# Packed attention's products grouped by tile shape, and a new order of the last batch, in a fused attention, MLP and expert kernel

## The chip, the cores and the metric

One core of a Trainium2 chip. The metric is device time in microseconds of one execution, all eight batches in one launch; the times given are medians of several executions. About 0.3% is what a measurement of this kernel can tell from no change.

## What is computed

The reference chains three layers over a batch of 8, with 576 tokens and 8 heads of 64 columns.

```python
p_packed = sm_attn(p, k, v)            # 32 packed rows per head
out = sm_attn(q, p_packed, p_packed)   # every token attends to the packed rows
...
h = gelu(x @ w_in); u, v = halves of h
gated = u * (w_sg @ layernorm(v) * g_ln + b_sg)
x = x + gated @ w_out
...
logits = x @ w_gate                    # 4 experts, the best 2 kept
for e in range(4):
    out += gate_e * softmax(causal(x @ wq[e] @ (x @ wk[e]).T / 8)) @ (x @ wv[e]) @ wo[e]
```

`sm_attn` is a softmax attention with its scores divided by the root of 64.

## The kernel before

**Batches overlap.** A batch b goes through `front(b)`: the products v and u of the MLP (lines 658 and 739), from the second attention's probabilities `a2` and from `wp`, which is the packed values times `w_in`. Then `back(b)` has the spatial product vs (L769), the query and key products qk (L825 and L837), values and gate logits vlog (L868, L872) and the gates. Expert attention of batch b runs as steps S0 to S9 (scores and softmax), T0 to T9 (transposes of the probabilities), y0 to y4 (times values) and o0 to o4 (times `w_o`, then stored). S and T are numbered 2j + pr: token tile j, expert pair pr. S8 and S9 are the last 64 tokens of the two pairs, and they read copies that `keep_last_q` makes on GpSimd. A batch's S0 and S2 come in its own `back`, all others run between the products of the next batch.

**The packed attention of batch b + 1** is laid between the products of `back(b)` as steps with letters, each for Q = 0 and 1 (four heads each). K turns keys to columns; s is the first scores with max and exponentials (L391, L478, L480); a transposes these (L494); p is the value product `pp` (L401: full-height tiles of 32 columns; L407: 32 by 32 tiles for the last 64 tokens) and its division; P transposes it (L420) and copies it out; Q joins the queries on GpSimd; r is the second scores (L391 again, tiles of 64 by 32), their softmax on VectorE, GpSimd and ScalarE, and the split of the result in a high and a low part. Every matrix product here is made of such parts, in three passes (`PASSES`).

`wp_mm(b + 1, f)` (L602, tiles of 64 by 32) multiplies the packed values by a half of `w_in`: f = 1 for v, f = 0 for u. `wp_out` copies it to a high part on ScalarE (L618) and a low part on VectorE (L623, in the rows as L85). These take two slots of tag "A" each; the four slots of "A" hold the gated values until the last key product, `qk_gated(b, 3, ...)`, has read them: two for m = 0 and 1, two for m = 2 and 3.

**What sets the order.** For TensorE (PE) and for the DMA queue of SyncE (SP) the order is the order of the program text, by hand. VectorE, ScalarE and GpSimd are ordered by a planner when the kernel is built: by priority, which is the order of the text (`s2_` is 150 places ahead), among the work that it takes to be ready. All PSUM tiles share four double banks (`pd`), given to a new tile when an older one has been read out.

**Loads of the packed attention's v.** Heads 4 to 7 of v (j = 2, 3) were loaded into the two "nat" slots, which hold heads 0 to 3 until `pp(0)` has read them. Four further small DMAs bring the last 64 tokens (`vr`, tag "rem", two slots): `load_nat` asks for one at j = 0 that nobody reads, `load_rest` for one each at Q = 0 and Q = 1, and `load_nat` at j = 2 for another that replaces the second.

```python
def p_(Q):                      # L571
    pp(Q)
    if Q == 0:
        for j in range(2, 4):
            load("v", v, j)
...
qk_gated(b, 3, False)           # L1161, in back
...
wp_out(b + 1, 1)
qk_out(b, 3)
wprime(b + 1, 0)                # wp_mm and wp_out
weights(b + 1, ("qk", "vg"))
```

`wp_mm(b + 1, 1)` stood ahead of this, at the end of `first_back` (batch 0) and of `later_back` (batches 1 to 7).

Of the kernel before, what the change touches and what calls it, by code (L numbers as in the profile page):

```python
# [7 lines left out]
F32 = mybir.dt.float32  # L8
# [9 lines left out]
P = 128  # L18
# [8 lines left out]
def packed_attention_mlp_moe_kernel(  # L27
# [43 lines left out]
    def nat_slot(dt, name):  # L71
        return sb.tile([P, 512], dt, tag="nat", name=name, bufs=NB["nat"])
# [281 lines left out]

    NAT = {}

    def load_nat(name, src, b, j):
        t = nat_slot(F32, name).rearrange("p (h n) -> p h n", h=2)
        off = (b * H + 2 * j) * S * D
        NAT[name, b, j] = t  # L360
        for h in range(2):
            nc.sync.dma_start(t[:, h].rearrange("p (c d) -> p c d", c=4),
                              dap(src, off + h * S * D, [[D, P], [P * D, 4], [1, D]]))
        if j % 2 == 0:
            r = small.tile([P, 2, D], F32, tag="rem", name=name + "r", bufs=2)
            for h in range(2):
                nc.sync.dma_start(r[:, h], dap(src, off + (512 + 32 * h) * D, [[S * D, 4], [D, 32], [1, D]]))
            NAT[name + "r", b, j // 2] = r.rearrange("p h d -> p (h d)")
# [9 lines left out]
    STEP = {}  # L378
    TURN = []

    def tick(n=1):
        for _ in range(min(n, len(TURN))):
            for f in TURN.pop(0):
                f()
# [42 lines left out]
    def p1_steps(b):  # L427
# [12 lines left out]
        def load(name, src, j):  # L440
            load_nat(name, src, b, j)
# [61 lines left out]
        def pp(Q):  # L503
            pp_mm_(b, Q, *s.pop(("a1T", Q)))
            pp_out(b, Q)
# [62 lines left out]
            for j in (2 * Q, 2 * Q + 1):  # L568
                join("q", j)

        def p_(Q):  # L571
            pp(Q)
            if Q == 0:
                for j in range(2, 4):
                    load("v", v, j)

        def s2_(Q):
            with tc.high_priority(offset=150):
                s2(Q)
                split_a2(b, Q)  # L580

        for n, fn in (("K", K), ("s", s1), ("Q", Q_), ("a", a1T), ("p", p_), ("P", ppT), ("r", s2_)):
            for Q in range(2):
                STEP[b, f"{n}{Q}"] = lambda fn=fn, Q=Q: fn(Q)
        return steps
# [25 lines left out]
    def wp_mm(b, f):  # L611
        pt = ST[b]["wpp", f] = pd("wp")
        per_head(b, pt, 512, w_of(b, f"in{f}"))
# [193 lines left out]
    def qk(b, i):  # L807
        qk_mm(b, i)
        qk_out(b, i)
# [3 lines left out]
        qk_gated(b, i, True)  # L813
        qk_packed(b, i, False)

    def qk_gated(b, i, first):
        s = ST[b]
        if first:
            s["qkp", i] = pd("qk")[:, :, :HALF]
        o = s["qkp", i]  # L820
        cols = slice(i * P, (i + 1) * P)
        for m in range(4):
            for x, y in PASSES:
                for h in range(2):
                    nc.tensor.matmul(o[:, h, :], W["w_qk"][y][:, m, cols], s["g", m][x][:, hs(h)],  # L825
                                     start=first and (m, x, y) == (0, 0, 0), stop=not first and (m, x, y) == (3, 1, 0))

    def qk_packed(b, i, first):
        s = ST[b]
        if first:  # L830
            s["qkp", i] = pd("qk")[:, :, :HALF]
        o = s["qkp", i]
        cols = slice(i * P, (i + 1) * P)
        for Q in range(2):
            for x, y in PASSES:
                for h in range(2):
                    nc.tensor.matmul(o[:, h, :], s["bd", Q][y][:, cols], s["a2", Q][x][:, hs(h)],  # L837
                                     start=first and (Q, x, y) == (0, 0, 0), stop=not first and (Q, x, y) == (1, 1, 0))

    def qk_out(b, i):  # L840
        s = ST[b]
        o = s.pop(("qkp", i))
        hi, lo = s["qk", i] = [slot("D", F32R, name="qk") for _ in range(2)]
        if i < 2:
            nc.scalar.activation(two(hi), o, AF.Copy, scale=0.125)  # L845
            nc.vector.scalar_tensor_tensor(two(lo), o, 0.125, two(hi).bitcast(F32), op0=OP.mult, op1=OP.subtract)
        else:
            nc.scalar.activation(two(hi), o, AF.Copy)
            lo_part(nc.vector, two(lo), o, two(hi))
# [236 lines left out]
    def first_back(b, do_all):  # L1086
        tick(len(TURN))
        do_all("K0")
        qk_gated(b, 0, True)
        do_all("s0 K1")  # L1090
        qk_gated(b, 2, True)
        do_all("s1")
        bdw(b)
        weights(b + 1, ("in1", "in0"))
        do_all("a0")
        qk_packed(b, 0, False)
        qk_out(b, 0)
        do_all("a1 p0 Q0")
        qk_packed(b, 2, False)
        qk_out(b, 2)  # L1100
        keep_last_q(b, 0)
        do_all("P0")
        vlog(b, VT[2])
        do_all("p1 r0 Q1 P1")
        vlog(b, VT[1])
        do_all("r1")
        wp_mm(b + 1, 1)
        ahead(b + 2)

    def later_back(b, go, do_all):  # L1110
        go("S1 S3")
        vs_tile(b, 0)
        vs_tile(b, 1)
        go("T1 T2 y0 S5 S4")
        vs_tile(b, 2)
        go("T3 o0 y1 T5 T4 S6 S7")
        vs_tile(b, 3)
        tick(len(TURN))
        if b + 1 < B:
            STEP.pop((b + 1, "f"))()  # L1120
        go("o1 y2")
        bdw(b)
        weights(b + 1, ("in1", "in0"))
        qk(b, 0)
        do_all("T6 o2 T7 K0 S8 S9 K1")
        keep_last_q(b, 0)
        qk(b, 2)
        do_all("y3 s0 s1 T8 T9 o3 a0 a1 y4 p0 Q0 Q1 o4 P0")
        vlog(b, VT[1])
        do_all("p1 r0 P1")  # L1130
        vlog(b, VT[2])
        do_all("r1")
        if b + 1 < B:
            wp_mm(b + 1, 1)
        if b + 2 < B:
            ahead(b + 2)

    def back(b, go):
        def do_all(names):

            for n in names.split():
                if (b + 1, n) in STEP:
                    STEP.pop((b + 1, n))()
                elif n[0] in "STyo":
                    go(n)

        if b:
            later_back(b, go, do_all)
        else:
            first_back(b, do_all)  # L1150
        nxt = attention(b)
        vlog(b, VT[0])
        tick()
        gates(b)
        qk(b, 1)
        keep_last_q(b, 1)
        tick()
        qk_packed(b, 3, True)
        tick()
        nxt("S0 S2" if b + 1 < B else "S8 S6")  # L1160
        qk_gated(b, 3, False)  # L1161
        tick()
        if b + 1 == B:
            qk_out(b, 3)
            return nxt
        wp_out(b + 1, 1)
        qk_out(b, 3)
        wprime(b + 1, 0)
        weights(b + 1, ("qk", "vg"))
        if b == 0:  # L1170
            for j in range(2):
                prep_w_o(j)
        return nxt
# [261 lines left out]
    with tc.manual_schedule(engines={ET.PE, ET.SP}):  # L1435
        go = back(0, attention(-1))
        for b in range(1, B):
            front(b, go)
            go = back(b, go)
        go("T8 S9 S7 T6 S4 T9 y4 S5 T7 o4 y3 S2 T4 S3 o3 T5 y2 S0 T2 S1 T3 o2 y1 T0 T1 o1 y0 o0")  # L1440


# [29 lines left out]
```

## Time and profile before

| | us |
|---|---|
| median of 3 runs (852.71 to 855.26) | 852.88 |
| the profiled execution, its device time | 852.21 |
| its span, first to last instruction | 850.4 |
| TensorE busy | 809.0 |
| VectorE busy | 583.6 |
| ScalarE busy | 432.8 |
| GpSimd busy | 227.0 |

The profiled execution is 0.67 below the median, and its device time is 1.8 above its span. Matmuls overlap in a row of the timeline: the cost of a group on TensorE is read from its start to the start of the next group, and not from its length. A row with an idle time in brackets names what ended it.

### The profile page before, as it was taken

To read this page: it belongs to the slowest core of one execution; us is meant where nothing else is said; L and a number is where in the kernel's file an instruction comes from. 1 tells how busy PE (TensorE), PEld (TensorE's weight loads), DVE (VectorE), ACT (ScalarE), POOL (GpSimd) and SP (SyncE) were. 2 spreads that over 40 slices of the span, in tenths; PEclk is the share of its full clock that TensorE was granted. 3 is DMA by queue.
4 is the path that set the end of the run, shared out by engine and by line. 5 is a ranking of instruction groups with operands and counts; after the bars stand their busy time and mean duration, and the time that the engine had idled before them with its cause. 6 is when DMAs were issued, how large, how long until landed. Compare 5 with 4: busy or idle time off the path is not lost.

```text
span 850.4 us, 19209 instructions
## 1 busy us (share of the span) xinstructions
PE 809.0 (95%) x7517; PEld 693.3 (82%) x7517; DVE 583.6 (69%) x1358; ACT 432.8 (51%) x983; POOL 227.0 (27%) x301
## 2 busy tenths in 40 slices
PE   5788989899999999999999999999999999999987
PEld 3456778789789888899789888898789888898965
DVE  5999445887488845876488745875489746875275
ACT  3665332665347542765347542765346542764255
POOL 2457422403322331403322331403322331300000
PEclk9999999999999999999999999999999999999999
DMA  9976886417655366528565476618563372000001
GB/s 255 275 193 166 220 250 166 131 59 207 137 154 125 95 201 139 168 47 228 121 160 113 100 195 136 163 55 237 121 159 106 95 202 84 26 13 27 19 1 57
DMA packets 172565, 114.99 MB, mean 135 GB/s; under 512 B 119290, under 2 KB 153338, under 8 KB 169660
## 3 DMA queue, kind: packets, MB, share of 16 engines
q1 hardware_dynamic: 165500, 112.19, 50.2%
q10 hardware_dynamic: 6976, 1.58, 0.9%
q8 instruction: 59, 0.97, 0.5%
q14 instruction: 30, 0.25, 0.1%
HBM read 69.18 MB, written 29.63 MB: 116 GB/s over the span
## 4 chain that ended last, share of the span: by engine, by line
PE 72%; DMA 11%; DVE 8%; SPq 3%; issue 2%; ACT 2%; POOL 1%; ACTq 0%; DVEq 0%; POOLq 0%
PE vs L769 12%; PE qk L825 9%; PE vlog L868 6%; PE o L1035 5%; PE u L739 5%; PE y L1004 5%; PE v L658 5%; PE qk L837 5%; DMA qp<-turned_q 4%; PE sc L921 4%; PE aTp L975 4%; PE vlog L872 3%; PE wp L602 2%; DMA w_in<-kept_in 1%; SPq L465 1%
## 5 line engine op out<-in xcount | busy, mean ns | idle before, releaser
L769 PE MATMUL vs<-w_sg,vnh 128*128 128x288 f32 x512 | 91.6, 301 | 1.5 <-ACT vs L82 1.5
L472 POOL COPY kT<-kp 128x576 uint16<-128x576 uint16 x56 | 51.1, 987 | 156.0 <-DMA kp<-turned_k 156.0
L825 PE MATMUL qk<-gh,w_qk 128*128 128x288 f32 x512 | 90.6, 299 | 0.0
L934 ACT ACTIVATE at<-sc,nm 128x256 f32<-128x256 f32 (+3 forms) x128 | 66.2, 525 | 39.5 <-DVE nm L925 34.6
L769 PEld LDWEIGHTS vs<-w_sg,vnh 128*128 128x128 f32 x512 | 74.5, 188 | 8.3 <-issue 3.3
L825 PEld LDWEIGHTS qk<-gh,w_qk 128*128 128x128 f32 x512 | 74.7, 188 | 4.7 <-issue 3.8
L82 ACT ACTIVATE aT<-aTp 128x512 f32<-128x512 f32 (+4 forms) x160 | 59.2, 434 | 21.7 <-PE aTp L975 21.2
L868 PE MATMUL vlog<-w_vg,gh 128*128 128x260 f32 (+1 forms) x320 | 61.1, 288 | 0.0
L1004 PE MATMUL y<-aT,v 128*64 128x128 f32 (+2 forms) x960 | 57.2, 262 | 0.8 <-ACT aT L82 0.8
L1004 PEld LDWEIGHTS y<-aT,v 128*64 128x64 f32 (+1 forms) x960 | 46.3, 136 | 13.3 <-issue 8.1
L938 DVE TENSOR_SCALAR at<-at,sm,gw 128x256 f32<-128x256 f32 (+3 forms) x128 | 55.3, 474 | 2.0
L676 POOL TENSOR_TENSOR rstd<-rstd,mhalf 128x1 f32<-128x1 f32 x40 | 35.5, 895 | 77.9 <-DVE rstd L672 74.5
L769 PE MATMUL vs<-w_sg,vnl 128*128 128x288 f32 x256 | 54.8, 296 | 1.0 <-POOL vnl L85 1.0
L472 POOL COPY qT<-qp 128x576 uint16<-128x576 uint16 x56 | 42.6, 833 | 47.2 <-DMA qp<-turned_q 47.1
L825 PE MATMUL qk<-gl,w_qk 128*128 128x288 f32 x256 | 54.9, 296 | 0.2 <-DVE gl L85 0.2
L855 POOL CAST last_q<-qk 64x64 fp32r<-64x64 f32 x64 | 14.9, 232 | 149.6 <-ACT qk L845 77.0
L925 DVE TENSOR_REDUCE nm<-sc 128x2 f32<-128x256 f32 (+3 forms) x64 | 52.7, 823 | 1.9
L1035 PE MATMUL o<-w_o,y 128*128 128x512 f32 x192 | 51.7, 404 | 1.4 <-ACT a L480 0.9
L868 PEld LDWEIGHTS vlog<-w_vg,gh 128*128 128x128 f32 (+1 forms) x320 | 47.7, 178 | 6.5 <-PE s L391 5.9
L874 ACT ACTIVATE v<-vlog 128x512 f32<-128x512 f32 (+1 forms) x24 | 12.6, 523 | 74.9 <-PE vlog L872 74.9
L837 PE MATMUL qk<-a2h,bdq 128*128 128x288 f32 x256 | 45.6, 301 | 0.0
L868 PE MATMUL vlog<-w_vg,gl 128*128 128x260 f32 (+1 forms) x160 | 45.1, 282 | 0.0
(234 smaller groups left out, 1972.0 us busy)
## 6 DMA issues: line engine op xcount, KB each, us to landing
w_in<-kept_in SPq DMA_DIRECT2D x14, 1024.0 KB
w_qk<-kept_qk SPq DMA_DIRECT2D x8, 1024.0 KB
out_dram<-ot SPq DMA_DIRECT2D x32, 256.0 KB
turned_k<-kx SPq DMA_DIRECT2D x28, 288.0 KB
turned_q<-qx SPq DMA_DIRECT2D x28, 288.0 KB
kp<-turned_k SPq DMA_DIRECT2D x56, 144.0 KB
qp<-turned_q SPq DMA_DIRECT2D x56, 144.0 KB
v<-in_v_dram SPq DMA_DIRECT2D x56, 128.0 KB
```

Of the source, the lines that this page charges most:

```text
L82: nc.scalar.activation(o, i, AF.Copy, scale=scale)
L472: nc.gpsimd.tensor_copy(w[:, i], t[:, i].rearrange("p h n -> p (h n)"))
L658: nc.tensor.matmul(pt, s["a2", Q][x][:, c * P:(c + 1) * P], wp_part(b, 1, y, Q), start=n == 0, stop=n == 5)
L769: nc.tensor.matmul(pt[:, h, :], s["vn", c][x][:, cols], w_sg[y][:, c, hs(h)], start=(c, x, y) == (0, 0, 0), stop=False)
L825: nc.tensor.matmul(o[:, h, :], W["w_qk"][y][:, m, cols], s["g", m][x][:, hs(h)], start=first and (m, x, y) == (0, 0, 0), stop=not first an ...
L837: nc.tensor.matmul(o[:, h, :], s["bd", Q][y][:, cols], s["a2", Q][x][:, hs(h)], start=first and (Q, x, y) == (0, 0, 0), stop=not first and ...
L868: nc.tensor.matmul(pt[:n, ci, :260], s["g", m][x][:, c * P:c * P + n], W["w_vg"][y][:, m, :], start=(m, x, y) == (0, 0, 0), stop=False)
L925: nc.vector.tensor_reduce(nm, pt[:, :, :L], axis=AX.X, op=OP.max, negate=True)
L934: nc.scalar.activation(ats[e][:, :L], pt[:, e, :L], AF.Exp, bias=nm[:, e:e + 1], accum_out=sm[:, e:e + 1])
L938: nc.vector.tensor_scalar(ats[e][:, :L], ats[e][:, :L], sm[:, e:e + 1], s["w"][:, j, 2 * pr + e:2 * pr + e + 1], op0=OP.mult, op1=OP.mult)
L1004: nc.tensor.matmul(pt[64 * e:64 * e + 64, pr * w:pr * w + w], s["v2"][:m, c, col:col + D], s["aT", pr, e, j][c][:m, :], start=c == 0, stop ...
L1035: nc.tensor.matmul(pt, ys[:, pr, x, :], W["w_o"][y][:, pr, :], start=i == 0, stop=i == 5)
```

## The change

- v of heads 4 to 7 goes to a slot of tag "a" (three slots, which hold expert probabilities, and in the start raw weights). It is a step of its own, V: after K1 in batch 0, and after T8 and T9 in the others.
- p1 directly follows p0 on TensorE in the batches after the first (Q0 and Q1 are GpSimd's), and P1 follows P0. In batch 0 p1 stays behind vlog of the last tile, and P1 follows it at once. r0 and r1 follow each other, behind vlog of tiles 2 and 3.
- s0 and s1 come before y3.
- `wp_mm` for f = 1 and f = 0 follow each other in the middle of the last key product, between its parts m = 0, 1 and m = 2, 3, with `wp_out` of f = 1 ahead of the second part and that of f = 0 behind the product.
- S0 and S2 come before the packed part of the last key product, not behind it.
- Last batch: S8 comes before qk 1, S6 before and S4 behind the packed part of the last key product, and the items behind it go in another order.

```diff
--- before.py
+++ after.py
@@ -354,8 +354,8 @@
 
     NAT = {}
 
-    def load_nat(name, src, b, j):
-        t = nat_slot(F32, name).rearrange("p (h n) -> p h n", h=2)
+    def load_nat(name, src, b, j, t=None):
+        t = (nat_slot(F32, name) if t is None else t).rearrange("p (h n) -> p h n", h=2)
         off = (b * H + 2 * j) * S * D
         NAT[name, b, j] = t
         for h in range(2):
@@ -568,18 +568,19 @@
             for j in (2 * Q, 2 * Q + 1):
                 join("q", j)
 
-        def p_(Q):
-            pp(Q)
-            if Q == 0:
-                for j in range(2, 4):
-                    load("v", v, j)
+        def V_():
+            t = slot("a", name="v")
+            for j in range(2, 4):
+                load_nat("v", v, b, j, t[:, (j - 2) * 512:(j - 1) * 512])
+
+        STEP[b, "V"] = V_
 
         def s2_(Q):
             with tc.high_priority(offset=150):
                 s2(Q)
                 split_a2(b, Q)
 
-        for n, fn in (("K", K), ("s", s1), ("Q", Q_), ("a", a1T), ("p", p_), ("P", ppT), ("r", s2_)):
+        for n, fn in (("K", K), ("s", s1), ("Q", Q_), ("a", a1T), ("p", pp), ("P", ppT), ("r", s2_)):
             for Q in range(2):
                 STEP[b, f"{n}{Q}"] = lambda fn=fn, Q=Q: fn(Q)
         return steps
@@ -813,13 +814,13 @@
         qk_gated(b, i, True)
         qk_packed(b, i, False)
 
-    def qk_gated(b, i, first):
+    def qk_gated(b, i, first, ms=range(4)):
         s = ST[b]
         if first:
             s["qkp", i] = pd("qk")[:, :, :HALF]
         o = s["qkp", i]
         cols = slice(i * P, (i + 1) * P)
-        for m in range(4):
+        for m in ms:
             for x, y in PASSES:
                 for h in range(2):
                     nc.tensor.matmul(o[:, h, :], W["w_qk"][y][:, m, cols], s["g", m][x][:, hs(h)],
@@ -1087,7 +1088,7 @@
         tick(len(TURN))
         do_all("K0")
         qk_gated(b, 0, True)
-        do_all("s0 K1")
+        do_all("s0 K1 V")
         qk_gated(b, 2, True)
         do_all("s1")
         bdw(b)
@@ -1101,10 +1102,9 @@
         keep_last_q(b, 0)
         do_all("P0")
         vlog(b, VT[2])
-        do_all("p1 r0 Q1 P1")
+        do_all("p1 Q1 P1")
         vlog(b, VT[1])
-        do_all("r1")
-        wp_mm(b + 1, 1)
+        do_all("r0 r1")
         ahead(b + 2)
 
     def later_back(b, go, do_all):
@@ -1125,13 +1125,10 @@
         do_all("T6 o2 T7 K0 S8 S9 K1")
         keep_last_q(b, 0)
         qk(b, 2)
-        do_all("y3 s0 s1 T8 T9 o3 a0 a1 y4 p0 Q0 Q1 o4 P0")
+        do_all("s0 s1 y3 T8 T9 V o3 a0 a1 y4 p0 Q0 p1 Q1 o4 P0 P1")
         vlog(b, VT[1])
-        do_all("p1 r0 P1")
+        do_all("r0 r1")
         vlog(b, VT[2])
-        do_all("r1")
-        if b + 1 < B:
-            wp_mm(b + 1, 1)
         if b + 2 < B:
             ahead(b + 2)
 
@@ -1152,20 +1149,30 @@
         vlog(b, VT[0])
         tick()
         gates(b)
+        if b + 1 == B:
+            nxt("S8")
+            qk(b, 1)
+            keep_last_q(b, 1)
+            nxt("S6")
+            qk_packed(b, 3, True)
+            nxt("S4")
+            qk_gated(b, 3, False)
+            qk_out(b, 3)
+            return nxt
         qk(b, 1)
         keep_last_q(b, 1)
         tick()
+        nxt("S0 S2")
         qk_packed(b, 3, True)
         tick()
-        nxt("S0 S2" if b + 1 < B else "S8 S6")
-        qk_gated(b, 3, False)
+        qk_gated(b, 3, False, (0, 1))
+        wp_mm(b + 1, 1)
+        wp_mm(b + 1, 0)
+        wp_out(b + 1, 1)
+        qk_gated(b, 3, False, (2, 3))
         tick()
-        if b + 1 == B:
-            qk_out(b, 3)
-            return nxt
-        wp_out(b + 1, 1)
         qk_out(b, 3)
-        wprime(b + 1, 0)
+        wp_out(b + 1, 0)
         weights(b + 1, ("qk", "vg"))
         if b == 0:
             for j in range(2):
@@ -1437,7 +1444,7 @@
         for b in range(1, B):
             front(b, go)
             go = back(b, go)
-        go("T8 S9 S7 T6 S4 T9 y4 S5 T7 o4 y3 S2 T4 S3 o3 T5 y2 S0 T2 S1 T3 o2 y1 T0 T1 o1 y0 o0")
+        go("T8 S2 T6 S9 S0 T4 S7 T9 y4 T2 S5 T7 o4 y3 T0 S3 T5 o3 y2 S1 T3 o2 y1 T1 o1 y0 o0")
 
 
 # ---- launch: one core; inputs and outputs as the reference has them ----
```

## Rows read from the trace of the kernel before

**Rows 1.** The page, part 1: busy time, share of the span, instructions.

```profile
PE 809.0 (95%) x7517; PEld 693.3 (82%) x7517; DVE 583.6 (69%) x1358; ACT 432.8 (51%) x983; POOL 227.0 (27%) x301
```

**Rows 2.** TensorE's waits, 100 to 780 us: in total, times, longest, us.

```profile
PE a1T L494 <- ACT a L480: 1.8, 6, 0.3
...
PE o L1035 <- ACT a L480: 0.9, 6, 0.2
```

**Rows 3.** TensorE's timeline of one batch: start us, length us, line, out<-in, tile, count.

```profile
310.79 1.20 PE L391 MATMUL s<-kT,pT 64*32 64x288 f32 x32
311.92 1.31 PE L989 MATMUL aTp<-ident,at 128*128 128x128 f32 x10
...
318.38 0.65 PE L401 MATMUL pp<-v,a1t 128*32 128x64 f32 x32
...
319.32 1.19 PE L1027 MATMUL o<-w_o,y 128*128 128x512 f32 x4
...
325.78 0.72 PE L391 MATMUL s<-qT,ppT 64*32 64x288 f32 x16
326.54 0.30 PE L420 MATMUL ppT<-ident,pp 128*128 128x128 f32 x1
...
328.91 0.72 PE L391 MATMUL s<-qT,ppT 64*32 64x288 f32 x16
329.42 1.06 PE L602 MATMUL wp<-w_in,ppT 64*32 64x512 f32 x16
330.42 0.51 PE L868 MATMUL vlog<-w_vg,gh 128*128 128x260 f32 x2
...
344.67 0.69 PE L825 MATMUL qk<-gh,w_qk 128*128 128x288 f32 x4
345.20 0.43 PE L825 MATMUL qk<-gl,w_qk 128*128 128x288 f32 x2
345.56 1.09 PE L602 MATMUL wp<-w_in,ppT 64*32 64x512 f32 x16
346.58 0.72 PE L658 MATMUL v<-wph,a2h 128*128 128x512 f32 x2
347.14 0.63 PE L658 MATMUL v<-wpl,a2h 128*128 128x512 f32 x2
```

**Rows 4.** TensorE's timeline: two products of 64 by 32 tiles that follow each other.

```profile
387.78 1.09 PE L602 MATMUL bdq<-w_qk,ppT 64*32 64x512 f32 x16
388.67 0.65 PE L602 MATMUL bdv<-w_vg,ppT 64*32 64x260 f32 x16
```

**Rows 5.** TensorE's timeline in batch 0: the second value product and what follows it.

```profile
128.08 0.30 PE L401 MATMUL pp<-v,a1t 128*32 128x64 f32 x4
...
130.41 0.71 PE L391 MATMUL s<-qT,ppT 64*32 64x288 f32 x16
```

**Rows 6.** TensorE's timeline: the second value product of a later batch, late.

```profile
610.64 1.13 PE L401 MATMUL pp<-v,a1t 128*32 128x64 f32 x32
```

**Rows 7.** The DMA queue of SP in the batch of rows 3.

```profile
302.56 6.33 SPq L465 DMA_DIRECT2D qp<-turned_q  x8
...
319.06 0.95 SPq L362 DMA_DIRECT2D v<-in_v_dram  x2
```

**Rows 8.** TensorE's waits in the last batch's tail, 803 to 851 us.

```profile
PE aTp L989 <- DVE at L960: 1.8, 1, 1.8
PE sc L951 <- DVE qk L85: 1.0, 1, 1.0
PE y L1004 <- ACT aT L82: 0.8, 1, 0.8
```

**Rows 9.** ScalarE's timeline ahead of v.

```profile
340.35 1.62 ACT L82 ACTIVATE a2h<-a2f 128x576 fp32r<-128x576 f32 x4
...
344.34 1.03 ACT L618 ACTIVATE wph<-wp 128x1024 fp32r<-128x1024 f32 x1
```

**Rows 10.** VectorE's timeline ahead of v.

```profile
345.63 1.22 DVE L85 TENSOR_TENSOR wpl<-wp,wph 128x1024 fp32r<-128x1024 f32 x1
```

## The prediction

> **What bounds the kernel now.** The page's busy table comes first: TensorE is busy for 809.0 of 850.4 us [rows 1], the next engine for 69%. So only two things can shorten the kernel: time that TensorE spends between its products, and the few stretches in which it waits. The list of its waits says how few those are in the middle of the kernel: the largest that come back batch after batch are a transpose (1.8 us in six batches) and an output product (0.9 us), both held by the exponentials of the first packed scores [rows 2]. The timeline of one batch comes next, read from start to start, for what a group costs that is waited for by nobody [rows 3, 4]; then the places where the change touches a load [rows 5 to 7], the tail [rows 8], and the copies that must be ready for the next batch's first product [rows 9, 10].
>
> **Second scores and w_in's products side by side.** The small-tile groups pay at their edges. The score group r1, which w_in's product follows with the same tile shape, takes 328.91 to 329.42 = 0.51 us; the group r0, which a full transpose follows, 325.78 to 326.54 = 0.76 [rows 3]. Together 1.27. Two score groups that stand side by side and leave to a full transpose are in the trace as s0 and s1: 310.79 to 311.92 = 1.13. So -0.14 in a batch. w_in's two products take 1.00 (329.42 to 330.42) and 1.02 (345.56 to 346.58) apart. A product of the same size that is followed by the same tile shape takes 387.78 to 388.67 = 0.89 [rows 4]; side by side they cost 0.89 + 1.02 = 1.91 instead of 2.02: -0.11.
>
> **Edges.** Four qk matmuls take 344.67 to 345.20 = 0.53, so two take 0.27; the last two before w_in's product take 345.20 to 345.56 = 0.36, or 0.09 more. Behind the product the first group of v is 0.72 long against 0.63 for the next, 0.09 again [rows 3]. The groups that move make four stretches of small tiles now (p0; p1 with r0; r1 with w_in; w_in) and three afterwards (p0 p1; r0 r1; w_in twice): one entry and one exit fewer, -0.18. Against that stands an edge that the trace does not show, from the 32 by 32 tiles at p0's end to the 32-column tiles at p1's start. It costs between nothing (tiles of one family) and 0.15; I take the 0.09 of an entry. Sum of this and the part before: -0.14 - 0.11 - 0.18 + 0.09 = -0.34 in a batch, -2.4 in seven.
>
> The rows say that a group which leaves its tile shape loses more than an entry, since the last tiles run out alone. The Trainium skill (TensorEngine Tiling (Array Packing), Key Properties) says that a change of tiling mode drains TensorE, and does not say more. By that rule, each value product has two modes in itself, so side by side saves them nothing inside: changes go from 11 to 9 in a batch, and with 0.09 each it would be -0.18, or -1.3 in seven, in place of -2.4.
>
> **v of heads 4 to 7 earlier.** In the batch of rows 3 a value product takes 318.38 to 319.32 = 0.94. In batch 0 the second one takes 128.08 to 130.41 = 2.33 [rows 5], as its v lands late: 1.39 lost. In one later batch its first part is 1.13 long against 0.65 [rows 6], 0.48 lost, and in one other the same. The load now has a slot of its own. SP issues the last query planes up to 302.56 + 6.33 = 308.9 [rows 7] and then V's six DMAs, ten microseconds ahead of 319.06, where v is issued now once p0 has let go of its slot; by the spacing of 0.95 for two they are out by 312 to 313, six ahead of p0. Behind them on SP stand the stores of o3 and o4, which are not ready then, and the next batch's transposes, whose place does not change. The slot of tag "a" was T7's or older, so SP does not stand at it. Gain 1.39 + 0.48 + 0.48 = 2.35, between 1.4 and 2.35.
>
> In batch 0 P1 now follows p1 at once, with the division between them; r0 (0.76) used to stand there. The wait is between 0 and 0.76; I take 0.6, as the division needs two VectorE instructions and two hand-overs. Batch 0 nets -0.8, the two later batches -1.0. In the other batches o4 stands between p1 and P1 (1.0 by rows 3, from 319.32 on), as it stands between p0 and P0 today, so no wait comes there. p1 needs the transposed probabilities 5.5 us sooner than today (325.78 - 0.94 against 319.32), but not sooner than p0's were ready; the copies are made in one go for both.
>
> **s0 and s1 before y3.** The exponentials start by the length of y3 earlier, and the work that covers them is the same plus y3. The waits of [rows 2] are 1.8 + 0.9 = 2.7. All of it can go. As much can come: s0's maximum then competes with the copies of qk 2 on VectorE and ScalarE, and y3's copies, due for o3, queue behind the exponentials. Bounds -2.7 and +2.7; I take -1.2, as the cover is the longer by y3 and the new conflicts are shorter.
>
> **Moved and costed at nothing.** S0 and S2 move past one product on TensorE. w_in's f = 1 product leaves its PSUM bank sooner. The query joins on GpSimd are begun behind p0 as before, so r1 finds them. The load of the next w_qk waits for w_in's f = 1 product, some 14 us later than now, and is due at the next batch's bdq at 387.78 [rows 4], 40 us later still. If that cover were gone, it would be a wait for a load of 1 MB.
>
> **The last batch.** TensorE waits 1.0 for the low part of the last key product before S9, 1.8 for S9's softmax before T9, and 0.8 for y2's operands [rows 8]. In the new order T8, S2 and T6 stand between the key product and S9, over 2 us of work, so the 1.0 goes. T9 has S0, T4 and S7 for cover, in place of S7, T6 and S4: about the same work, but VectorE has S4's softmax behind it. I take 0.2 of the 1.8. y2 finds more softmax done: 0.6 of 0.8. Sum -1.8, between 0 and -3.6.
>
> **The sum.** -2.4 - 0.8 - 1.0 - 1.2 - 1.8 = -7.2. The profiled execution took 852.21, so 845.0; the median of the runs shown is 0.67 above it, so **845.7 us**.
>
> **Rivals.** *The waits eat the gain.* Placing s0 before y3 puts +2.7 in place of -1.2, and the last batch gives nothing as VectorE is its bound: -2.4 - 0.8 - 1.0 + 2.7 = -1.5, 851.4, no change. For it: the four engines of that stretch are ordered by a planner that the change does not address. Against it: [rows 2] are short waits, and cover grows.
>
> *v waits for w_in's high part, slower.* Today ScalarE makes w_in's f = 1 high part at 344.34, 2.2 before v [rows 3, 9], with the product long done. Afterwards the product ends about 1.1 (its row's length) after it starts, and v starts 0.89 + 1.02 + 1.7 (half a key product's gated part, twelve matmuls at 0.13, with its edge) = 3.6 after. The high part (1.03) and the low part (1.22) [rows 9, 10] end at 3.4 if both engines are free; the low part is needed half a microsecond into v (346.58 to 347.14), so 0.7 is to spare. If ScalarE puts the copies of a2 (1.62) and the exponentials of S0 and S2 (about as long, an estimate) in between, high and low come 3.2 late, and v stands for 2.5. Seven times that is 17.5, less 7.2: 863. It decides from 0.7 + 7.2/7 = 1.7 of delay. Against it: a2's copies need only the packed product, which now ends before the first half.
>
> *SP stands at the last 64 tokens, slower.* V asks for a third piece of `vr` beside two slots. If it got the slot that p0 still has to read, SP would stand until p0's end, and p1, now right behind, would wait for two small loads, the rest of v and their landing: four issues at about 0.5 [rows 7], and a landing that I estimate to be as long again, 4 us. Seven times 4 is 28: 874. It decides by which slot is handed out. Against it: the slot that nobody reads is free by then.
>
> **How the numbers follow.** The forecast has 0.80, the eaten gain 0.10, the late high part 0.06, the standing queue 0.04. The bounds of the forecast: at best -3.0 (no inner edge), -1.4, -1.0, -2.7, -3.6, which is 840.5 on the profiled scale; at worst -1.3 by edges alone, -0.6, 0, 0, 0: 850.3. Against the median that is 841.2 to 851.0. All of these at once is unlikely at the fast end, so the range starts at 842.0; it ends at 851.2, which takes in most of the forecast and part of the eaten gain. A difference of 0.3%, or 2.6 us, is about what can be told from no change: below 850.3 is faster, above 855.4 slower. Faster 0.79, same 0.11, slower 0.10.
>
> **What the changed profile would show.** Right: p0 to o4 takes about 1.9 from start to start with no bracket on the value product; r0 and r1 together 1.1 to 1.2; w_in's two 1.9; a first vlog group without an edge behind vlog of tile 4; no wait ahead of S9 in the tail; a steady batch shorter by some 0.5. Wrong: a wait of v for the high or low part of w_in, an SP stretch that stands inside V's six DMAs, an o3 that waits for exponentials by more than today's 0.2 [rows 2], or a T9 that waits for 3 us.

## The result: 1.1% slower, and where the time lies in the profile after

The changed kernel takes **862.26 us** (median of 4; 861.18 to 864.47) against 852.8 (852.28 to 855.26): ratio 1.0109, interval 1.0081 to 1.0137. The forecast was 845.7 us, with a range from 842.0 to 851.2: the sign is wrong.

The page's head and first table of the changed kernel, as in [rows 1]:

```profile
span 860.7 us, 19233 instructions
...
PE 808.9 (94%) x7517; PEld 694.5 (81%) x7517; DVE 585.2 (68%) x1358; ACT 432.5 (50%) x983; POOL 229.6 (27%) x301
```

TensorE's busy time is that of before to 0.1 us, and the span is 10.3 longer. Summed over the kernel, the difference is waiting. In the last batch alone it is not: there TensorE is busy for longer, as the tail below shows, by about as much as it is busy for less in the rest. I read the spans from bdq to bdq, the first product of a batch. From one to the next: 95.1 before (95.6 in the two batches with a late v), 96.6 after. In parts of the two spans: the start +0.8, batch 0 -1.7 (83.2 to 81.5), six batches +8.2 (571.5 to 579.7), the last bdq to the end +3.0 (81.3 to 84.3); sum 10.3.

The list of TensorE's waits of the changed kernel (total, times, longest), which answers to [rows 2] and [rows 8]:

```profile
PE v L659 <- DVE wpl L85: 8.6, 7, 1.8
...
PE o L1036 <- ACT y L1015: 6.7, 7, 1.0
PE aTp L990 <- DVE at L961: 3.5, 1, 3.5
```

The first comes in every batch: v's second product waits for the *low* part of w_in's first half, which VectorE makes. The second is the wait of o3 for y3's copy, 6.2 in six batches in place of the 0.9 and 1.8 of before (the seventh, 0.5, stands in the tail of both kernels). The third is T9's in the tail.

The batch that answers to [rows 3], on TensorE, from its bdq to the next:

```profile
293.28 1.09 PE L603 MATMUL bdq<-w_qk,ppT 64*32 64x512 f32 x16
...
314.85 1.68 PE L1036 MATMUL o<-w_o,y 128*128 128x512 f32 x6 [1.03 <-ACT y L1015]
...
319.09 0.65 PE L401 MATMUL pp<-v,a1t 128*32 128x64 f32 x32
...
320.97 1.19 PE L1028 MATMUL o<-w_o,y 128*128 128x512 f32 x4
...
326.60 1.20 PE L391 MATMUL s<-qT,ppT 64*32 64x288 f32 x32
327.73 0.46 PE L869 MATMUL vlog<-w_vg,gh 128*64 128x260 f32 x2
...
343.39 1.09 PE L603 MATMUL wp<-w_in,ppT 64*32 64x512 f32 x16
344.70 1.09 PE L603 MATMUL wp<-w_in,ppT 64*32 64x512 f32 x16 [0.23 <-ACT at L935]
...
347.41 0.63 PE L659 MATMUL v<-wph,a2h 128*128 128x512 f32 x2
349.19 0.73 PE L659 MATMUL v<-wpl,a2h 128*128 128x512 f32 x2 [1.15 <-DVE wpl L85]
...
389.93 1.09 PE L603 MATMUL bdq<-w_qk,ppT 64*32 64x512 f32 x16
```

p0 and p1 take 1.88 side by side, r0 and r1 1.13, as forecast. The largest loss stands in v's second product. VectorE in the same stretch:

```profile
327.61 0.85 DVE L519 STREAM_TRANSPOSE bt<-s 128x288 f32<-128x288 f32 x2
...
331.31 0.75 DVE L530 TENSOR_REDUCE sm<-bt 128x18 f32<-128x576 f32 x1 [2.06 <-ACT bt L524]
...
333.63 0.78 DVE L535 STREAM_TRANSPOSE a2f<-bt 128x576 f32<-128x576 f32 x1
334.33 0.81 DVE L519 STREAM_TRANSPOSE bt<-s 128x288 f32<-128x288 f32 x2
...
341.12 0.43 DVE L923 TENSOR_TENSOR sc<-sc,causal 128x256 f32<-128x256 f32 x1
341.59 0.76 DVE L847 SCALAR_TENSOR_TENSOR qk<-qk 128x576 fp32r<-128x576 f32 x1
342.26 0.77 DVE L535 STREAM_TRANSPOSE a2f<-bt 128x576 f32<-128x576 f32 x1
...
344.69 1.43 DVE L936 TENSOR_SCALAR sm<-sm 128x2 f32<-128x2 f32 x1 [0.42 <-ACT at L935]
...
347.92 2.35 DVE L85 TENSOR_TENSOR wpl<-wp,wph 128x1024 fp32r<-128x1024 f32 x2
```

The same two turns of r1, its first and its last, in the kernel before (bdq at 292.69):

```profile
333.14 0.81 DVE L519 STREAM_TRANSPOSE bt<-s 128x288 f32<-128x288 f32 x2
...
339.01 0.78 DVE L535 STREAM_TRANSPOSE a2f<-bt 128x576 f32<-128x576 f32 x1
```

In the changed kernel the scores of r1 lie ready at 327.8. VectorE first finishes r0, stands for 2.06 while GpSimd and ScalarE work on it, and turns r1 at 334.33, 6.5 later. The gates come ahead of r1's sum, S0's mask and qk 1's low part ahead of its last turn. Counted from bdq this last turn starts at 49.0, before at 46.3, 2.7 earlier. Then come S0's and S2's scalings, and at last w_in's low parts in one go, 347.92. v wants the first of them at 348.0.

A steady batch can be added up from this: v's wait 1.15, w_in's second product 0.23, and 1.03 for o3 in place of 0.16 and 0.31 for o3 and the transposes, less 0.37 of edges (below), is 1.6; the batches got 1.5 longer.

### The profile page after: what moved, and what is told of

It reads as the page before. It is cut to its first block, busy times and chain, and to the rows that moved or that the text cites. A ratio compares the mean times of both kernels' runs of the same rounds, so it can differ in the third digit from the quotient of the medians.

```text
span 860.7 us, 19233 instructions
## 1 busy us (share of the span) xinstructions
PE 808.9 (94%) x7517; PEld 694.5 (81%) x7517; DVE 585.2 (68%) x1358; ACT 432.5 (50%) x983; POOL 229.6 (27%) x301
## 3 DMA queue, kind: packets, MB, share of 16 engines
q1 hardware_dynamic: 165500, 112.19, 49.9%
## 4 chain that ended last, share of the span: by engine, by line
PE 61%; DVE 14%; ACT 3%; DMA 3%; issue 3%; POOL 1%; SPq 0%; DVEq 0%; ACTq 0%; POOLq 0%
PE vs L770 11%; PE y L1005 6%; PE v L659 5%; PE o L1036 5%; PE u L740 5%; PE qk L826 5%; PE aTp L976 4%; PE sc L922 4%; PE vlog L869 3%; DMA qp<-turned_q 3%; PE qk L838 3%; PE vlog L873 2%; DVE bt L519 1%; DVE mx L522 1%; DVE sm L530 1%
## 5 line engine op out<-in xcount | busy, mean ns | idle before, releaser
L856 POOL CAST last_q<-qk 64x64 fp32r<-64x64 f32 x64 | 18.4, 288 | 143.6 <-ACT qk L846 62.9
L523 POOL TENSOR_TENSOR bt<-bt,mx 128x576 f32<-128x576 f32 x14 | 16.7, 1193 | 109.6 <-DVE mx L522 71.2
L976 PE MATMUL aTp<-ident,at 128*128 128x128 f32 x320 | 45.3, 280 | 0.0
```

The costliest lines, as they stand in the source:

```text
L976: nc.tensor.transpose(pt[:, e, c * P:c * P + P], ats[e][:, c * P:c * P + P], ident)
```

## Experiments

All are edits of the changed kernel, named by what they undo or add. Behind `s2_`, line numbers are those of before plus 1, with run 8's edit plus 8. "Per batch" is bdq to bdq of the steady batches of the profiled execution, "tail" from the last bdq to the end. These tell more than the medians, since the start up to the first bdq alone lies anywhere from 112.1 to 118.9 us in these profiles. Ratios are to the kernel before on the same chip.

**1. The last batch in the old order.**

```diff
         if b + 1 == B:
-            nxt("S8")
...
-            nxt("S6")
...
-            nxt("S4")
+            nxt("S8 S6")
...
-        go("T8 S2 T6 S9 S0 T4 S7 T9 y4 T2 ...
+        go("T8 S9 S7 T6 S4 T9 y4 S5 ...
```

> The changed kernel with the last batch's old order (S8 and S6 behind the packed part of the last key product, and the old list behind it); all else as changed. Theory: of the 9.4 us, the new order of the last batch costs 3 (T9 waits for 3.5 us, the granted clock halves behind it for 10 us, and 4 us are gained elsewhere in the tail), so 862.3 - 3 = 859.2, T9's wait back at about 1.8, no half clock in the tail, and the steady batch still 96.7 us. Rival: the tail is longer because the batch ahead of it ends with its engines behind, so the old order waits as long and the time stays at 862.

864.1 us, 1.0126 (1.0104 to 1.0148); 96.55 per batch, tail 84.7. The theory missed by 5, and the old list does not bring the old tail back: S4's mask and maximum (830.33, 830.79) now stand ahead of S9's scaling (831.66) on VectorE, where before they stood behind it (823.07 and 823.53, the scaling 822.58), and T9 waits 2.4 where it waited 1.8. The rival has the time, but not its reason: S9's mask starts 49.8 us after the last bdq in both kernels, so the engines do not come late out of the batch ahead. The order of VectorE, not TensorE's list by itself, sets the tail.

**2. w_in's two products apart again** (the last lines in batch 0 too).

```diff
...
-        qk_gated(b, 3, False, (0, 1))
-        wp_mm(b + 1, 1)
-        wp_mm(b + 1, 0)
-        wp_out(b + 1, 1)
-        qk_gated(b, 3, False, (2, 3))
+        qk_gated(b, 3, False)
...
+        wp_out(b + 1, 1)
         qk_out(b, 3)
-        wp_out(b + 1, 0)
+        wprime(b + 1, 0)
...
         do_all("r0 r1")
+        if b + 1 < B:
+            wp_mm(b + 1, 1)
...
```

> The changed kernel with w_in's two products where they stood (f = 1 behind r1, f = 0 behind the last key product), all else as changed. Theory A (the wait of v for w_in's low part, 1.2 us in each of seven batches, comes from the late place of the f = 1 product): the wait is gone, the steady batch goes from 96.7 to 95.3, the time to about 853. Theory B (VectorE and ScalarE are late themselves, since the two second scores side by side leave VectorE idle while GpSimd and ScalarE have the first one, and put the second one's softmax behind the gates): v still waits for 0.8 us or more, for a2's copies or for w_in's low part, and the time stays above 857.

874.49 us, 1.0257 (1.0219 to 1.0295); 97.4 to 98.2 per batch. A new wait takes the first place of the list:

```profile
PE qk L838 <- DVE qk L847: 14.8, 7, 3.5
```

The packed product waits for a PSUM bank, which is free when VectorE has made qk 1's low part (L847). It is the same VectorE queue, met at another place. Theory A missed; theory B had the sign but not the place: v's own wait for the low part is down to 0.8 in all.

**3. S0 and S2 behind the packed product, as before.**

```diff
-        nxt("S0 S2")
         qk_packed(b, 3, True)
         tick()
+        nxt("S0 S2")
```

> The changed kernel with S0 and S2 back behind the packed part of the last key product, all else as changed. Theory C (S0's mask and the key product's low part stand ahead of the last turn of the second softmax on VectorE because S0 comes earlier): that turn ends 0.8 us sooner and v's wait falls from 1.2 to 0.4, the time to 857. Theory A or B: S0's and S2's exponentials and scalings come later instead and stand ahead of w_in's copies all the same, v's wait stays at 1.0 or more, the time at 861 to 864.

856.0 us, 1.002 (0.9995 to 1.0045); 95.4 per batch, v waits 0.26, as theory C had it. VectorE in the batch whose bdq is at 292.67:

```profile
341.08 0.77 DVE L535 STREAM_TRANSPOSE a2f<-bt 128x576 f32<-128x576 f32 x1
...
346.05 1.22 DVE L85 TENSOR_TENSOR wpl<-wp,wph 128x1024 fp32r<-128x1024 f32 x1
```

The last turn now stands ahead of S0's mask, 48.4 after bdq in place of 49.0, and w_in's first low part starts at 53.4 in place of 54.6. So the move that the prediction cost at nothing is worth 1.2 in a batch.

**4. y3 ahead of s0, as before.**

```diff
-        do_all("s0 s1 y3 T8 T9 V ...
+        do_all("y3 s0 s1 T8 T9 V ...
```

> The changed kernel with y3 ahead of s0 and s1 again, all else as changed. Theory: o3's wait of 1.0 for y3's copy, which stands behind both exponentials on ScalarE, falls to 0.2, and the wait of the transposes for the exponentials comes back at 0.3; from y3 or s0 to y4's start a batch takes 7.85 now and took 7.74 before, so six batches gain 0.7: 861.6. Rival: the wait of o3 is one more microsecond in each batch, and the time falls by 5, to 857.

860.41 us, 1.0074 (1.0037 to 1.0112). o3's wait is 0.2 again, and v's stays (9.2 in seven): the theory's time, not the rival's.

**5. Both moves undone:** the diffs of runs 3 and 4 together.

> S0 and S2 behind the packed product and y3 ahead of s0, both as in the kernel before; the grouped value products, the late pair of w_in's products and the new last batch stay. Theory A (the two moves are what lengthens a batch: 96.6 us from bdq to bdq after, 95.1 before): without S0's move a batch took 95.43, and y3's copy ahead of the exponentials takes the 1.03 wait of o3 out, so about 95.2 and 854 us; v waits 0.3 at most. Rival B (the late pair is the cost, since its low part on VectorE cannot be ready for v): v still waits 1 us or more in a batch, 96 and 860 us.

858.93 us, 1.005 (1.0025 to 1.0075); 95.4 per batch, 95.9 in two where w_in's product waits for a bank. v waits 0.3. Theory A's batch was right to 0.2, its time 5 too low: the tail is 2.1 longer than before, and the start with batch 0 is 2.6 longer. And the batch is still no gain on before: the grouping's own 0.3 is missing.

**6. The value products and second scores side by side alone:** the diffs of runs 1 to 4 together.

> Only the value products side by side, the second scores side by side and v of heads 4 to 7 in its own slot; S0's and y3's places, w_in's two products and the last batch as before. Theory A: the grouping is worth what it measured from y4 to qk 1 in the changed kernel, 0.27 in a batch (1.9 in all), plus 1.7 in batch 0 and 1.0 for the two late loads: 4.6 below the kernel before, 849 us, 94.8 in a batch. Rival: the grouping gains nothing by itself, because the engines behind it (division, transposed copies, softmax of the second scores) are the bound of that stretch: 95.1 in a batch, and only batch 0 and the late loads give something, 851 us.

876.46 us, 1.0269 (1.022 to 1.0319); 96.4 to 99.3 per batch: both theories missed by far. The list of waits, then VectorE and GpSimd at the place:

```profile
PE sc L922 <- DVE qk L847: 16.0, 7, 4.2
```

```profile
347.32 1.08 DVE L903 TENSOR_SCALAR gsm<-gsm 128x5 f32<-128x5 f32 x1
...
348.76 0.75 DVE L847 SCALAR_TENSOR_TENSOR qk<-qk 128x576 fp32r<-128x576 f32 x1
```

```profile
346.97 1.69 POOL L85 TENSOR_TENSOR a2l<-a2f,a2h 128x576 fp32r<-128x576 f32 x2
```

S2 waits for the bank that qk 1's low part frees (348.76, 49.9 behind bdq; before 47.8). r1's turn is again behind the whole of r0, 40.7 behind bdq, as before, though its scores were made 2.5 us sooner. So I took neither an early r1 nor the moves for the common root, but VectorE's order of the two softmaxes, which became theory A of run 8.

**7. S0 and S2 behind w_in's two products, y3 first** (the diff of run 4 as well).

```diff
-        nxt("S0 S2")
         qk_packed(b, 3, True)
...
         wp_out(b + 1, 1)
+        nxt("S0 S2")
         qk_gated(b, 3, False, (2, 3))
```

> S0 and S2 stand behind w_in's two products, ahead of the second half of the gated product, so that the planner has w_in's first high and low part ahead of their softmax; y3 ahead of s0; the rest as changed. Theory A: v waits for nothing; S0 and S2 have lost no cover that T0 needs (it comes 20 us later); 95.0 in a batch, 853 us. Rival B: w_in's low part still comes late as VectorE is busy with the gates and the last turn, v waits 1 us: 96 and 860 us.

859.79 us, 1.007 (1.0044 to 1.0096); 95.8 per batch. v does not wait, as theory A had it, but the time is the rival's, since S0 waits:

```profile
PE sc L922 <- DVE wpl L85: 7.7, 7, 1.1
```

The wait for the low part has only moved to a bank. Whatever TensorE's order, it meets the end of the same chain.

**8. Both score tiles turned first.** One edit to the changed kernel, in `s2_`:

```diff
         def s2_(Q):
+            if Q == 0:
+                return
             with tc.high_priority(offset=150):
-                s2(Q)
-                split_a2(b, Q)
+                for i in range(2):
+                    s2_mm(i)
+                for i in range(2):
+                    s2_exp(i)
+                for i in range(2):
+                    s2_norm(i)
+                    split_a2(b, i)
```

> The changed kernel with one edit: VectorE turns both second score tiles and takes both maxima before it sums either, where the changed kernel finishes r0 (with 2.06 us of idle VectorE) and only then turns r1 (with the gates in a second gap). Theory A (VectorE's chain from the second scores to w_in's low part sets when v starts): the last turned result comes some 2 us earlier, v's wait of 1.15 in a batch goes, 95.4 us from bdq to bdq and 853 us. Rival (the low part stands behind S0's and S2's scaling in any case, which wait for the exponentials): v still waits 0.8 or more, 96.3 and 860 us.

**853.28 us**, 0.9985 (0.9962 to 1.0008), by the ratios 1.2% below the changed kernel; 94.84 per batch, 1.8 less, as theory A had it and better. All 7517 products of TensorE stand in the same order in both kernels. VectorE, and v's second product, of this kernel (bdq at 293.82):

```profile
328.16 0.85 DVE L519 STREAM_TRANSPOSE bt<-s 128x288 f32<-128x288 f32 x2
...
329.71 0.84 DVE L519 STREAM_TRANSPOSE bt<-s 128x288 f32<-128x288 f32 x2
...
331.86 0.75 DVE L530 TENSOR_REDUCE sm<-bt 128x18 f32<-128x576 f32 x1 [0.52 <-ACT bt L524]
...
336.67 0.78 DVE L535 STREAM_TRANSPOSE a2f<-bt 128x576 f32<-128x576 f32 x1
...
346.64 1.22 DVE L85 TENSOR_TENSOR wpl<-wp,wph 128x1024 fp32r<-128x1024 f32 x1
```

```profile
347.98 0.67 PE L666 MATMUL v<-wpl,a2h 128*128 128x512 f32 x2
```

The idle 2.06 is 0.52, the last turn stands 42.9 behind bdq in place of 49.0, and the low part is done 0.1 before v wants it: no bracket on v, though S0, S2 and w_in stand as in the changed kernel. (In batch 0 alone v still waits 1.8.)

**9. The same, and y3 ahead of s0:** the diffs of runs 8 and 4.

> The same edit, and y3 ahead of s0 as before. Theory A: also o3's wait of 1.03 for y3's copy goes and about 0.3 of waits for exponentials comes, so another 0.4 in a batch: 95.0 and 850 us. Rival: as without the edit to the turns, 96 and 859 us.

852.64 us, 0.9964 (0.994 to 0.9988); 94.72 per batch, 0.37 below before. y3's move cost 0.12 in a batch, less than the 0.4 expected here: it trades waits of 0.3 and 0.2 for one of 1.0, less what the neighbours save.

**10. The grouping alone, with both tiles turned first:** the diffs of runs 6 and 8.

> The value products and second scores side by side alone, with both turns first (without that edit a batch took 98.0, as S0 waited up to 4.2 us for a bank behind a late copy of qk 1 on VectorE). Theory A (the grouping makes VectorE's chain later and its own saving is sound): S0's wait goes, 94.8 in a batch, 852 us with the old tail. Rival (w_in's product, held in its bank from r1 to the end of the last key product, is what S0 waits for): 97 in a batch, 868 us.

852.79 us, 0.9996 (0.9972 to 1.002); 94.69 per batch against 96.4 to 99.3. Theory A: in the steady batches the bank held by w_in's product was not the cause. The total is held up by its tail (84.7) and one wait of 3.0 in batch 0. Beside run 12, which has S0 and y3 in the same places, it shows that w_in's move gains nothing by itself (94.69 without, 94.72 with it).

**11. The tail: T9 behind four items.** Run 5 and

```diff
-            qk_gated(b, 3, False)
+            qk_gated(b, 3, False, (0, 1))
+            nxt("S2")
+            qk_gated(b, 3, False, (2, 3))
...
-        go("T8 S2 T6 S9 S0 T4 S7 T9 y4 T2 S5 ...
+        go("T8 T6 S9 S0 T4 S7 S5 T9 y4 T2 ...
```

> As the run without the two moves, but S2 between the halves of the last gated product and the last items as T8 T6 S9 S0 T4 S7 S5 T9 y4 T2 T7 and so on, so that T9 has four items behind S9 in place of three and S2's softmax is over by then. Theory A (T9's 3.5 us wait stands for VectorE's queue, and the half clock behind it for the wait): wait of T9 under 1 us, no half-clock stretch, tail 3.5 plus about 2.5 shorter than 83.7, 848 us. Rival (S5's mask and maximum take the place of S2's, and S9's scaling comes as late as before): T9 waits 2 us or more, half clock stays, 853 us.

855.41 us, 1.0013 (0.9989 to 1.0037); tail 82.7. T9 waits 2.3, and the granted clock is halved for 6.8 us behind it. Mostly the rival (2 us or more, the half clock stays), though by another tile: S7's maximum (826.74, 1.21 long) stands ahead of S9's reciprocal and scaling.

**12. All even scores ahead of the last product's end,** with the diffs of runs 5 and 8.

```diff
-            nxt("S6")
+            nxt("S6 S4")
             qk_packed(b, 3, True)
-            nxt("S4")
-            qk_gated(b, 3, False)
+            nxt("S2")
+            qk_gated(b, 3, False, (0, 1))
+            nxt("S0")
+            qk_gated(b, 3, False, (2, 3))
...
-        go("T8 S2 T6 S9 S0 T4 S7 T9 y4 ...
+        go("T8 T6 S9 S7 T4 S5 T9 y4 T7 ...
```

> Both turns first, S0 and S2 behind the packed product, y3 ahead of s0, and another last batch: S8, S6, S4, S2, S0 all between the last key products, then T8 T6 S9 S7 T4 S5 T9 y4 T7 and so on, so that VectorE has only odd tiles to scale behind the last product. Theory A: 95.0 in a batch (v's 0.26 and the 1.0 of two batches go), T9 waits under 1 us and the half clock behind it goes, tail 79 to 80 in place of 83.4: 849 us. Rival for the tail (VectorE is full there whatever the order): T9 waits 2 us or more, tail 83, 853 us.

852.09 us, 0.9974 (0.9956 to 0.9993); 94.72 per batch as theory A had it, tail 81.6: T9 waits 2.6 and 3.4 us of half clock follow, as the rival had it.

**13. T2 and T0 ahead of T9 as well.** Run 9, the even scores as in run 12 (S0 and S2 of the other batches ahead of the packed product, as in the changed kernel), and

```diff
-        go("T8 S2 T6 S9 S0 T4 S7 T9 y4 T2 S5 T7 o4 y3 T0 S3 ...
+        go("T8 T6 S9 S7 T4 T2 S5 T0 T9 y4 T7 o4 y3 S3 ...
...
-            t = slot("A", name="aT")
+            t = slot("A" if j > 1 else "a", name="aT")
...
```

> Both turns first and y3 ahead of s0 (94.72 in a batch), S0 and S2 ahead of the packed product, and a last batch in which S8, S6, S4, S2 and S0 stand between the last key products and the items behind it run T8 T6 S9 S7 T4 T2 S5 T0 T9 y4 T7 o4 and so on; T2 and T0 take slots of tag a, so that four transposes of even tiles can stand ahead of T9. Theory A: with 1 us more of work between S9 and T9, and S9's scaling right behind S7's maximum on VectorE, T9's wait falls from 2.6 to under 1 and no half clock follows it; tail 79, 849 us, faster than the kernel before. Rival: T9 waits 2 us or more, tail 82, 852 us.

**847.27 us, 0.9911 (0.9889 to 0.9933): faster than both kernels.** TensorE, then VectorE, of its tail:

```profile
823.76 0.75 PE L997 MATMUL aTp<-ident,at 128*128 128x128 f32 x5 [0.56 <-DVE at L968]
824.64 1.82 PE L1012 MATMUL y<-aT,v 128*64 128x64 f32 x40
826.39 1.11 PE L983 MATMUL aTp<-ident,at 128*128 128x128 f32 x8
```

```profile
821.51 1.22 DVE L933 TENSOR_REDUCE nm<-sc 128x2 f32<-128x1024 f32 x1
...
823.03 0.58 DVE L968 TENSOR_SCALAR at<-at,sm,wl 128x576 f32<-128x576 f32 x1
823.53 0.42 DVE L930 TENSOR_TENSOR sc<-sc,causal 128x256 f32<-128x256 f32 x1
```

T9 waits 0.56, S9's scaling stands ahead of S5's mask, and the tail is 78.7, as theory A had it. Per batch it is 95.05 in this profile, whose granted clock is 0.95 throughout (1.00 in the middle of run 9), so 0.3 in a batch may be that execution's.

The changed kernel's tail beside it: TensorE, VectorE, and two stretches by engine (PE, PEld, DVE, ACT and POOL: busy times and counts, then the granted clock):

```profile
832.49 1.30 PE L990 MATMUL aTp<-ident,at 128*128 128x128 f32 x5 [3.52 <-DVE at L961]
833.72 2.99 PE L1005 MATMUL y<-aT,v 128*64 128x64 f32 x40
836.64 1.11 PE L976 MATMUL aTp<-ident,at 128*128 128x128 f32 x4
```

```profile
830.44 1.22 DVE L926 TENSOR_REDUCE nm<-sc 128x2 f32<-128x1024 f32 x1
831.57 0.15 DVE L960 RECIPROCAL sm<-sm 128x1 f32<-128x1 f32 x1
...
831.76 0.58 DVE L961 TENSOR_SCALAR at<-at,sm,wl 128x576 f32<-128x576 f32 x1
```

```profile
822.00:831.40 9.40, 6.97 (x57) 5.68 (x55) 8.46 (x23) 6.80 (x21) 0.00 (x0) 1.00 0.00 1
831.40:841.60 10.20, 9.11 (x66) 7.32 (x67) 4.47 (x13) 4.16 (x12) 0.00 (x0) 0.50 0.01 2
```

VectorE is busy for 8.46 of the 9.40 us ahead of T9. S9's scaling waits behind S7's maximum, T9 for the scaling, and then the clock is 1.2 GHz for 10.2 us: y4 takes 833.72 to 836.64 = 2.92, in run 13 824.64 to 826.39 = 1.75. The whole tail, first of the kernel before, then of the changed one:

```profile
769.10:850.40 81.30, 72.59 (x652) 62.22 (x650) 38.91 (x108) 35.83 (x95) 1.86 (x8) 0.99 0.08 27
```

```profile
776.40:860.70 84.30, 75.97 (x652) 65.06 (x650) 38.75 (x108) 36.34 (x95) 1.87 (x8) 0.94 0.08 26
```

With the same 652 products TensorE is busy for 3.4 longer, and stands for 0.4 less. So the longer tail is the half clock's, not that of the waits by themselves.

## Why the prediction was wrong, point by point

**Right: the edges.** The sum -0.34 in a batch is there once VectorE does not eat it: 94.72 in run 9 against 95.09, -0.37. Summed from start to start over one batch, before and run 9: vlog 11.18 and 10.99, second scores with the first 2.40 and 2.26, w_in 2.01 and 1.88, qk 19.66 and 19.75, v 6.95 and 6.90, transposes of the packed values 0.08 and 0.14. The inner edge from p0 to p1, bounded by 0 and 0.15 (a bound that no row gave) and taken at 0.09, is nothing that these rows show: 0.94 each, as alone. The terms are less sure than their sum: run 10, with w_in's products apart, gets the same 94.69, since there r1 again stands in front of w_in's product (second scores with the first 2.12, w_in 2.02). Counting changes of mode alone, by the rule of the Trainium skill that the prediction weighed (TensorEngine Tiling (Array Packing), Key Properties), gave -0.18; the runs show twice that, which fits the prediction's reading that a group which leaves its shape loses more than an entry (0.25 between r0 and r1 in [rows 3]).

**Right: v's load.** Late v is gone in the later batches (the value products take 1.88 in place of 2.38 in one of them, 0.50 against the 0.48 forecast), SP does not stand in V's six DMAs, and P1 waits 0.7 in batch 0, forecast 0.6. That batch 0 came out 1.7 shorter for a forecast of 0.8 is not these terms alone: S0's wait of 2.4 in it went, and one of v (1.8) and one of w_in (1.0) came.

**Wrong, the step that decided: "S0 and S2 move past one product on TensorE", cost nothing.** The same holds for r0 and r1, whose cover was GpSimd's joins ("so r1 finds them"). Both were costed on TensorE; what they hand to VectorE was not placed. Between the second scores and v, the chain through VectorE is the bound, and it had 0.3 of slack before: w_in's first low part started at 345.63 and took 1.22 [rows 10], to 346.85, and v's second product started at 347.14 [rows 3]. Run 3 prices S0's move at 1.2 in a batch, run 6 shows that the grouping alone loses through the same chain, and run 8 takes the loss out by an edit to the order of the softmax's steps, with TensorE's order untouched. That is the cause of the longer batch, shown by adding and taking away.

**The rival "v waits for w_in's high part"** had the place, v, at a chance of 0.06, with the wrong reason: it let ScalarE put other work ahead of the high part, and gave the low part 0.7 to spare "if both engines are free". VectorE was not free. That its 863 lies so near the measured time is luck: it had v stand for 2.5 in a batch with the rest of the gain kept, while v stood for 1.15, and the rest of the loss came from o3 and the tail. The low part came late by 1.15, and by 0.26 with S0 where it was.

**Wrong: s0 and s1 before y3.** -1.2 in a kernel was taken from bounds of -2.7 and +2.7; by runs 8 and 9 the move costs 0.12 in a batch, 0.7 in six. ScalarE got both exponentials (the second at 313.69) ahead of y3's copy, and o3 waited 1.0:

```profile
314.42 0.38 ACT L1015 ACTIVATE y<-y 128x256 fp32r<-128x256 f32 x1
```

"y3's copies, due for o3, queue behind the exponentials" stood among the prediction's bounds and was not taken.

**Wrong: the last batch.** -1.8 was +3.0. The 1.0 ahead of S9 went, as said, and so did the 0.8 of y2. But T9's cover was counted in TensorE's work, "about the same work, but VectorE has S4's softmax behind it": in the new order S0's, S2's and S7's masks and maxima stand ahead of S9's scaling, and T9 waits 3.5 in place of 1.8. In waits that still comes out even. The loss is the half clock behind T9's wait, which was in no term. Nor is it the new list's alone: with the old list and the other edits the tail is as long (84.7, 84.3 and 84.7 in runs 1, 6 and 10, T9 waiting 2.4 in each). Run 13, which mends that queue, has a tail of 78.7, 5.6 below the changed kernel's.

**What stays open.** How the 1.8 that run 8 gains splits between the idle VectorE and what GpSimd held (below) was not tried. Why the planner orders the old list's tail otherwise than in the kernel before was not found.

## What to carry to other kernels

A gap on TensorE closes only if what is due behind it is ready: before moving a product, follow its *result* through the engines that a planner orders, to the next thing that waits for it, and count the slack there. Two softmaxes in a row on VectorE with a detour over other engines should be written maximum, maximum, sum, sum, not one after the other: here that was worth 1.8 us in a batch. At the end of a kernel, order the list by the last engine of the chain and look at the granted clock behind every longer wait.

## What the runs showed of the hardware

**A wait can cost twice.** Behind T9's wait in the tail the granted clock fell to 1.2 GHz at about the wait's end (831.4 in the changed kernel, whose T9 starts at 832.49). In the changed kernel and in runs 7 to 9 (a wait of 3.5) that lasted 10.2 us, in runs 2 to 5 (3.5 as well) 6.8, in runs 1, 6, 10 and 11 (2.4, and 2.3 in the last) 6.8, and in run 12 (2.6) 3.4; in the kernel before (1.8) and in run 13 (0.56) the clock did not fall there. In runs 2 and 6, stretches of 3.4 at 1.2 GHz stand in four and in five of the six steady batches too. Why the stretches differ in length was not tried.

**A tiny VectorE instruction stands while GpSimd subtracts.** An instruction on 128x2 takes 0.16 us elsewhere in the same profile (346.87) and 1.43 while GpSimd makes a2's low part (344.69 above, to 346.11; of GpSimd's four instructions in this row the third stands from 344.66 to 346.09):

```profile
343.00 3.38 POOL L85 TENSOR_TENSOR a2l<-a2f,a2h 128x576 fp32r<-128x576 f32 x4
```

In the same way one of 128x5 takes 1.08 in run 6, where it delays qk 1's low part. The reciprocals and the reductions that stand beside this work of GpSimd keep their length (in the changed kernel 0.17 for a reciprocal of 128x2, and 0.41 for a reduction of 128x256 that takes 0.43 elsewhere). The Trainium skill (SBUF — State Buffer, SBUF: two separate sides) says that VectorE, in some instructions, and GpSimd take turns at one pair of ports, held for a whole instruction; these rows agree, and no run here took GpSimd's work away to test it.
